# A new scheduler model and joined attention calls in a one-core kernel of attention and two mixture layers

## The chip, the cores and the metric

The kernel runs on one core of a Trainium2 chip. The metric is the device time of one execution in microseconds (us); lower is better. A core has TensorE (PE: matmuls, with its weight loads shown apart as PEld), VectorE (DVE), ScalarE (ACT), GpSimd (POOL) and SyncE (SP), which here issues all DMA transfers in one queue.

## The reference

Attention in 64 chunks of 64 by 64 for each of 8 heads, then two dense layers with gates; everything is fp32.

```python
B, H, S, D = 8, 8, 576, 64            # 4608 tokens, 512 wide
scores = matmul(q_c, k_c.T) / sqrt(D) # per 64-token chunk and head
attn = exp(scores - max); attn /= sum + 1e-9
x = matmul(attn, v_c)                 # -> [4608, 512]
g = x @ w_gate; v = x @ w_val         # [512, 1536] each
y = (g * sigmoid(g) * v) @ w_out      # [1536, 512]
h = y @ w_in                          # [512, 2048]
out = (h * sigmoid(1.702 * h)) @ w_out2   # [2048, 512]
```

## The kernel before

The 4608 tokens are cut into 9 blocks of 512. The work runs in four passes over all blocks: two over halves of the first layer (three groups of weights each), two over halves of the second (two groups each). A group multiplies a block by seven combinations of its quarters instead of eight quarters (`product`, seven calls a group, labels 1 to 7), and every fp32 factor is split into a high and a low part, so that a product is three matmuls (`mm3`, lines 249, 250 and 251: these are most of the time). One `product` call is twelve matmuls of 128x128 by 256 columns. What follows a group on PE is `second` in the first layer (three matmuls of 512 columns) and `last_product` in the second (six of 256 columns). In the second layer all seven products of a group go through one PSUM bank, `ga`; between two of them ACT copies the bank away (`u` or `c`, line 233).

Attention is part of the first pass: while block b is multiplied, `attend` makes the 4 units (128 tokens each) of block b+1. A unit is a score call on PE (16 small matmuls of 64x64 in the source, 32 rows in the trace, into bank `s`, line 483), a softmax of six DVE instructions and one exp on ACT (lines 488 to 496), four transposes on PE (line 507), a copy, a value call on PE (line 483 again, into bank `a`) and a copy into `xr`. `x_made` then splits the block into the seven x tiles.

The weights come as 8-byte numbers. `conv_part` turns them to fp32 (two ACT and two DVE instructions, lines 328 to 336), and splits by ACT and POOL follow. The first groups are made at the start (tiles `w`); those of later passes are background work (tiles `raw`, `t`, `st`, `ws`) that is stored in device memory and loaded later. In the second layer's last pass the second group's output weights are loaded one by one into the ring `o`, which has three buffers; ring `w` has 21.

Nothing is issued in the order in which it is written. Each step is an `Op` with an engine, a guessed duration, a priority (`prio`, a planned time in us) and its dependencies; `Program.emit` walks a model of the engines forward in time, takes on each engine the ready step of lowest priority and so fixes the order of every engine's queue and of SP's. On the chip each queue then runs in that order, and an instruction waits for its inputs.

```python
s, o = min(((s, o) for s, o in zip(start, todo) if s <= first + (0.1 if eng == "dve" else 0.3)),
           key=lambda x: (x[1].prio, x[1].n))
```

Of the kernel before, what the change touches and what calls it, by code (L numbers as in the profile page):

```python
# [18 lines left out]
P = 128  # L19
# [7 lines left out]
class Buf:  # L27
# [3 lines left out]
    def __init__(self, make, prev=None, before=None, whole=None):  # L31
        self.make, self.prev, self.before, self.whole = make, prev, before, whole
        self.users, self.writers, self.tile = [], [], None
# [18 lines left out]
class Ring:  # L52
    def __init__(self, pool, tag, bufs):
        self.pool, self.tag, self.bufs, self.made = pool, tag, bufs, []

    def new(self, shape, dtype=F32):
# [4 lines left out]
        b = Buf(make, prev, self.made[-1] if self.made else None)  # L61
        self.made.append(b)
# [3 lines left out]
class Op:  # L66
    __slots__ = ("eng", "us", "fn", "prio", "deps", "follows", "table", "near", "n", "done_at")


class Program:  # L70


    def __init__(self):
        self.ops, self.slack = [], None

    def op(self, eng, us, fn, reads=(), writes=(), prio=0, table=None, near=None):
        o = Op()
        o.eng, o.us, o.fn, o.prio, o.table, o.near, o.n = eng, us, fn, prio, table, self.slack if near is None and eng not in ('pe', 'dma') else near, len(self.ops)
# [20 lines left out]
    def emit(self):  # L99
        waiting = {o: len(o.deps) + len(o.follows) for o in self.ops}  # L100
        after = {}
        for o in self.ops:
            for d in (*o.deps, *o.follows):
                after.setdefault(d, []).append(o)
        ready = {}
        for o in self.ops:
            o.done_at = 0.0
            if not waiting[o]:
                ready.setdefault(o.eng, []).append(o)
        free, table = {}, None  # L110
        left = len(self.ops)
        while left:
            pick = None
            for eng, todo in ready.items():
                if not todo:
                    continue
                t = free.get(eng, 0.0)
                start = [max(t, o.done_at) for o in todo]
                first = min(start)
                s, o = min(((s, o) for s, o in zip(start, todo) if s <= first + (0.1 if eng == "dve" else 0.3)), key=lambda x: (x[1].prio, x[1].n))  # L120
# [4 lines left out]
            free[o.eng] = s + o.us + (1.3 if o.table and o.table != table else 0.0)  # L125
            end = free[o.eng] + (2.0 if o.eng == "dma" else 0.0)
            table = o.table or table
            o.fn()
            left -= 1
            for a in after.get(o, ()):  # L130
                if o in a.deps:
# [861 lines left out]
```

## Time and profile before

| | |
|---|---|
| median of 3 runs (lowest to highest) | 1752.32 us (1750.62 to 1753.2) |
| the profiled execution | 1753.21 us, of which its span (first to last instruction) is 1751.4 us |
| PE busy | 1704.3 us, 97% of the span |
| DVE, ACT, POOL busy | 1111.5 us, 882.3 us, 735.2 us |
| DMA | 477.91 MB, mean 273 GB/s |
| mean granted clock of PE | 0.987 of full speed |

A busy PE is not PE at its peak: the records of matmuls overlap, so the distance from one start to the next is the better measure of pace. Idle time of the other engines costs nothing as long as PE doesn't wait for them.

### The profile page before, as it was taken

To read this page: it belongs to the slowest core of one execution; us is meant where nothing else is said; L and a number is where in the kernel's file an instruction comes from. 1 tells how busy PE (TensorE), PEld (TensorE's weight loads), DVE (VectorE), ACT (ScalarE), POOL (GpSimd) and SP (SyncE) were. 2 spreads that over 40 slices of the span, in tenths; PEclk is the share of its full clock that TensorE was granted. 3 is DMA by queue.
4 is the path that set the end of the run, shared out by engine and by line. 5 is a ranking of instruction groups with operands and counts; after the bars stand their busy time and mean duration, and the time that the engine had idled before them with its cause. 6 is when DMAs were issued, how large, how long until landed. Compare 5 with 4: busy or idle time off the path is not lost.

```text
span 1751.4 us, 36463 instructions
## 1 busy us (share of the span) xinstructions
PE 1704.3 (97%) x14392; PEld 1617.2 (92%) x14392; DVE 1111.5 (63%) x1632; ACT 882.3 (50%) x1535; POOL 735.2 (42%) x762
## 2 busy tenths in 40 slices
PE   6889999999999999999999999999999999999998
PEld 6779989889999999999999989999999999999997
DVE  6887678767774464544445548778775555555555
ACT  5776666666763343333333446555544444444442
POOL 4665464636652145212222235656662133333333
PEclk8989999999999999999999999999999999999999
DMA  6568888887869988777778998989989977777774
GB/s 246 188 230 279 289 293 280 270 270 276 295 229 366 331 290 292 260 251 246 254 258 281 352 353 279 320 288 312 310 299 321 364 248 227 218 233 232 228 223 137
DMA packets 187323, 477.91 MB, mean 273 GB/s; under 512 B 20112, under 2 KB 47760, under 8 KB 187152
## 3 DMA queue, kind: packets, MB, share of 16 engines
q1 hardware_dynamic: 187152, 475.58, 80.5%
q8 instruction: 114, 1.87, 0.4%
q14 instruction: 57, 0.47, 0.1%
HBM read 334.46 MB, written 141.03 MB: 271 GB/s over the span
## 4 chain that ended last, share of the span: by engine, by line
PE 86%; DVE 5%; ACT 2%; issue 2%; DMA 1%; POOL 0%; POOLq 0%; ACTq 0%; DVEq 0%
PE ga L249 11%; PE ga L251 10%; PE ga L250 10%; PE yb L249 4%; PE ya L250 4%; PE ya L249 4%; PE ya L251 4%; PE yb L251 4%; PE yb L250 4%; PE gb L249 4%; PE gb L251 4%; PE gb L250 4%; PE s L249 2%; PE s L251 2%; PE s L250 2%
## 5 line engine op out<-in xcount | busy, mean ns | idle before, releaser
L249 PE MATMUL ga<-x,w 128*128 128x256 f32 x1640 | 472.9, 288 | 10.9 <-ACT u L233 3.9
L250 PE MATMUL ga<-x,w 128*128 128x256 f32 x1640 | 463.9, 283 | 3.0 <-DVE x L242 3.0
L251 PE MATMUL ga<-x,w 128*128 128x256 f32 x1640 | 464.6, 283 | 0.4 <-POOL w L242 0.4
L249 PEld LDWEIGHTS ga<-x,w 128*128 128x128 f32 x1640 | 311.7, 190 | 26.7 <-ACT u L233 9.8
L250 PEld LDWEIGHTS ga<-x,w 128*128 128x128 f32 x1640 | 311.6, 190 | 8.2 <-DVE x L242 3.3
L251 PEld LDWEIGHTS ga<-x,w 128*128 128x128 f32 x1640 | 311.5, 190 | 0.6 <-POOL w L242 0.6
L233 ACT COPY u<-ga 128x512 f32<-128x512 f32 x231 | 135.3, 586 | 254.3 <-PE ga L251 252.1
L242 DVE TENSOR_TENSOR c<-u,ga 128x512 f32<-128x512 f32 x143 | 98.2, 687 | 239.1 <-PE ga L251 229.7
L653 ACT ACTIVATE xr<-c 128x512 f32<-128x512 f32 x140 | 88.3, 631 | 135.1 <-DVE c L242 128.2
L242 DVE TENSOR_TENSOR c<-u,gb 128x512 f32<-128x512 f32 x125 | 85.4, 683 | 95.7 <-ACT u L233 68.0
L249 PE MATMUL gb<-x,w 128*128 128x256 f32 x500 | 143.4, 287 | 1.5 <-DVE c L242 1.5
L251 PE MATMUL gb<-x,w 128*128 128x256 f32 x500 | 141.8, 284 | 0.0
L250 PE MATMUL gb<-x,w 128*128 128x256 f32 x500 | 141.6, 283 | 0.0
L613 ACT ACTIVATE h<-c 128x512 f32<-128x512 f32 x108 | 67.9, 632 | 118.6 <-DVE c L242 118.0
L235 POOL CAST ws<-t 128x256 fp32r<-128x256 f32 x78 | 41.0, 526 | 193.7 <-DMA wd_b<-ws 85.5
L242 DVE TENSOR_TENSOR xr<-xr 128x512 f32<-128x512 f32 x140 | 117.4, 839 | 5.4 <-ACT xr L653 3.1
L242 POOL TENSOR_TENSOR k<-xr,q 128x512 fp32r<-128x512 f32 x24 | 37.5, 1564 | 173.8 <-ACT q L233 64.7
L242 DVE TENSOR_TENSOR hl<-h,hh 128x512 fp32r<-128x512 f32 x108 | 92.0, 872 | 17.0 <-ACT hh L233 16.8
L249 PEld LDWEIGHTS gb<-x,w 128*128 128x128 f32 x500 | 95.4, 191 | 4.3 <-DVE c L242 1.7
L242 POOL TENSOR_TENSOR u<-u 128x512 f32<-128x512 f32 x36 | 48.7, 1352 | 117.7 <-ACT u L233 117.7
L242 POOL TENSOR_TENSOR yv<-yv,e 128x512 f32<-128x512 f32 x18 | 23.2, 1288 | 177.2 <-ACT e L233 115.9
L250 PEld LDWEIGHTS gb<-x,w 128*128 128x128 f32 x500 | 95.5, 191 | 2.0
(253 smaller groups left out, 5077.0 us busy)
## 6 DMA issues: line engine op xcount, KB each, us to landing
x<-x_dram SPq DMA_DIRECT2D x189, 512.0 KB, 5.3
o<-od_b SPq DMA_DIRECT2D x126, 512.0 KB, 4.7
o<-od_a SPq DMA_DIRECT2D x102, 512.0 KB, 5.3
x_dram<-x SPq DMA_DIRECT2D x63, 512.0 KB, 4.3
wd_b<-ws SPq DMA_DIRECT2D x56, 256.0 KB, 5.0
od_b<-ws SPq DMA_DIRECT2D x56, 256.0 KB, 5.1
w<-wd_b SPq DMA_DIRECT2D x28, 512.0 KB, 6.2
raw<-in_moe_w_out SPq DMA_DIRECT2D x56, 255.8 KB, 4.8
```

The lines of the kernel that those rows point to most:

```text
L233: op("act", act_us(n), lambda: nc.scalar.copy(out=dst.ap, in_=cut(src.ap)), [src], [dst], prio, near=near)
L235: op("pool", pool_us(0.6 * n), lambda: nc.gpsimd.tensor_copy(dst.ap, cut(src.ap)), [src], [dst], prio)
L242: lambda: e.tensor_tensor(out=dst.ap, in0=of_a(a.ap), in1=of_b(b.ap), op=by), [a, b], [dst], prio, near=near)
L249: nc.tensor.matmul(o, ah, bh, start=first, stop=False, **kind)
L250: nc.tensor.matmul(o, ah, bl, start=False, stop=False, **kind)
L251: nc.tensor.matmul(o, al, bh, start=False, stop=last, **kind)
L613: op("act", act_us(512), lambda h=h, i=i: nc.scalar.activation(out=h.ap, in_=of(0)(c[i].ap), func=AF.Silu), [c[i]], [h], prio, "silu")
L653: op("act", act_us(512), lambda: nc.scalar.activation(out=h.ap, in_=c.ap, func=AF.Gelu_apprx_sigmoid), [c], [h], prio, "gelu")
```

## The change

Three things. First, the durations given to the steps are new, and the model now knows that DVE and POOL share a port (`port`: a DVE step that reads no PSUM tile, and every POOL step, take it one after the other), how long a hop between engines lasts, and how transfers queue. Second, `emit` runs 12 rounds: it makes an order (`order`), works back from its end to the latest time at which each step may end or begin (`dues`), steps through the order once more with a model of PE's clock (`replay`), and then moves each step's key half way to its latest time; the best of the 12 by `replay` is issued. Third, attention from block 2 on is cut otherwise: `attend_next` makes units two ahead of the block, and `scores` issues the value call of unit u-2 and the score call of unit u as one step (`both_blocks`); units 34 and 35 end with a value call alone. There are 26 joined calls. And in the last block of the last pass the `o` tiles of the second group come from ring `w`.

```diff
     def op(self, eng, us, fn, reads=(), writes=(), prio=0, table=None, near=None, port=None):
...
+        o.port = eng == "pool" or eng == "dve" and port is not False and not any(a.bank for b in reads for a in b.line())
...
+    def order(self):
...
+                limit = min(max(t, o.ready) for o in todo) + self.WINDOW[eng]
+                o = min((o for o in todo if o.ready <= limit), key=lambda o: (o.key, o.n))
...
+                if o.port:
+                    o.end = max(s + 0.1, port) + o.us - 0.1
+                    port = o.end - 0.1
+                else:
+                    o.end = s + o.us
...
+    def dues(self, seq):
...
+            if o.eng == "dma":
+                o.due = t - 2.8 - 0.865 * o.us
+            elif o.eng == "pe":
+                o.due = free = min(t, free) - o.us
+            else:
+                o.due = t - o.us
...
+    def emit(self):
+        for o in self.ops:
+            o.key, o.after = o.prio, []
...
+        for i in range(self.ROUNDS):
+            seq = self.order()
+            self.dues(seq)
+            last = self.replay(seq)
+            if best is None or last < best[0]:
+                best = last, seq
+            for o in self.ops:
+                if o.prio < 9999:
+                    o.key = (o.key + o.due) / 2
+        for o in best[1]:
             o.fn()
...
+    def scores(un, prio, done=None):
+
+        if done is None:
+            op("pe", 1.24, lambda: blocks(un.s.ap, un.q.ap, un.k.ap), [un.q, un.k], [un.s], prio)
+        else:
+            def both_blocks():
+                blocks(done.o.ap, done.v.ap, done.e.ap)
+                blocks(un.s.ap, un.q.ap, un.k.ap)
+
+            op("pe", 2.2, both_blocks, [done.v, done.e, un.q, un.k], [done.o, un.s], prio, near=1.0)
+            attended(done, prio)
...
+    def attend_next(u, prio):
+
+        if u < NU:
+            un = unit(u)
+            fetch(un, un.q, q, prio - 10)
+            fetch(un, un.k, k, prio - 10)
+            scores(un, prio, flying.pop(0) if len(flying) > 1 else None)
+            softmax(un, prio)
+            flying.append(un)
+        else:
+            alone(flying.pop(0), prio)
+        last = [un for un in flying if un.v is None and un.u < u]
+        for un in last:
+            un.v = ring["v"].new([P, 512])
+            fetch(un, un.v, v, prio - 6)
+            turned(un, prio)
...
-                                        w = ws[n] = ring["o"].new([P, 2, 2, 256], F32R)
+                                        tag = "w" if (p, b) == (NPASS - 1, NB - 1) else "o"
+                                        w = ws[n] = ring[tag].new([P, 2, 2, 256], F32R)
...
-                    for u in range(UPB * j // len(gs), UPB * (j + 1) // len(gs)):
-                        at = t - 22 + u * 14 if b else t + 4 + u * 16
-                        attend(UPB * (b + 1) + u, at, at - 10)
+                    units = range(2 if b > 1 else 0, UPB + 2 if b else UPB)
+                    for u in units[len(units) * j // len(gs):len(units) * (j + 1) // len(gs)]:
+                        if b:
+                            attend_next(UPB * (b + 1) + u, t + -6.0 + (u - 2) * 13.5)
+                        else:
+                            attend(UPB + u, t + 4 + u * 16, t - 6 + u * 16)
```

How this moves the instructions is seen at three places.

DVE while block 0 is multiplied, before: the rows that lead to the end of the conversion of the third group's first weight tile (lines 333 and 336, `t`); lines 488 to 496 are a unit's softmax, `c` an evacuation that PE waits for.

```order
L489 TENSOR_TENSOR e<-s,m 128x512
L492 TENSOR_REDUCE z<-e 128x8
L242 TENSOR_TENSOR c<-u,gb 128x512
L493 TENSOR_SCALAR z<-z 128x8
L495 RECIPROCAL z<-z 128x8
L496 TENSOR_TENSOR e<-e,z 128x512
L333 SCALAR_TENSOR_TENSOR t<-t,raw 128x256
L242 TENSOR_TENSOR c<-u,ga 128x512
L336 SCALAR_TENSOR_TENSOR t<-raw,t 128x256
L333 SCALAR_TENSOR_TENSOR t<-t,raw 128x256
L242 TENSOR_TENSOR c<-u,gb 128x512
L336 SCALAR_TENSOR_TENSOR t<-raw,t 128x256
```

The same after the change, to the same conversion's end (lines 452 and 455; the softmax has lines 630 to 638).

```order
L361 TENSOR_TENSOR c<-u,gb 128x512
L361 TENSOR_TENSOR h<-h,c 128x512
L630 TENSOR_REDUCE m<-s 128x8
L452 SCALAR_TENSOR_TENSOR t<-t,raw 128x256
L455 SCALAR_TENSOR_TENSOR t<-raw,t 128x256
L361 TENSOR_TENSOR hl<-h,hh 128x512
L631 TENSOR_TENSOR e<-s,m 128x512
L452 SCALAR_TENSOR_TENSOR t<-t,raw 128x256
L455 SCALAR_TENSOR_TENSOR t<-raw,t 128x256
```

The conversion's last row stood as DVE's 99th instruction and stands as its 86th; the conversions that follow it move ahead by 14 to 19, and softmaxes move behind them. By the evacuation of the fifth product of block 1's first group 165 instructions stood ahead on DVE, now 159: one unit's softmax is no longer among them. The background conversions of later weights move too: before the last evacuation of the first pass's last group 176 of 256 conversion instructions stood on DVE, now 192, and before block 8's last x tile 237 of 447 background steps stood on POOL, now 285.

PE in the last pass, before: between two products through `ga` (their last and first rows) there is one `last_product` (into bank `s`).

```order
L250 MATMUL ga<-x,w 128x256
L251 MATMUL ga<-x,w 128x256
L249 MATMUL s<-w,v 128x256
L250 MATMUL s<-w,v 128x256
L251 MATMUL s<-w,xt 128x256
L249 MATMUL s<-w,v 128x256
L250 MATMUL s<-w,v 128x256
L251 MATMUL s<-w,xt 128x256
L249 MATMUL ga<-x,w 128x256
```

After, ahead of the same product (its first row stands last), the end of two `last_product` calls (into `ya`).

```order
L369 MATMUL ya<-w,hh 128x256
L370 MATMUL ya<-w,hl 128x256
L368 MATMUL ya<-w,hh 128x256
L369 MATMUL ya<-w,hh 128x256
L370 MATMUL ya<-w,hl 128x256
L368 MATMUL ya<-w,hh 128x256
L369 MATMUL ya<-w,hh 128x256
L370 MATMUL ya<-w,hl 128x256
L368 MATMUL ga<-x,w 128x256
```

In the second layer's passes 32 products stood one `last_product` behind the product before them in `ga`, 178 two, 27 three or more; now 1, 228 and 8. Products right behind each other in `ga` are 4 before and 4 after.

SP at the end, before: the last loads of output weights (`o`, from the second group's `od_b`), among the stores of the last blocks' outputs.

```order
L226 DMA t<-o_dram 128x512
L226 DMA o<-od_b_96 128x1024 x3
L229 DMA out<-yv 128x2x256
L226 DMA o<-od_b_96 128x1024
L229 DMA out<-yv 128x2x256
L229 DMA out<-t 128x2x256 x2
```

SP at the end, after.

```order
L345 DMA w<-od_b_96 128x1024
L345 DMA yv<-o_dram 128x512
L345 DMA o<-od_b_96 128x1024
L345 DMA w<-od_b_96 128x1024 x2
L348 DMA out<-yv 128x2x256
L348 DMA out<-t 128x2x256
L345 DMA yv<-o_dram 128x512
L345 DMA t<-o_dram 128x512
L348 DMA out<-t 128x2x256
L348 DMA out<-yv 128x2x256 x2
L348 DMA out<-t 128x2x256 x2
```

The seven loads that go into `w` (the last three are shown) stand ahead of the stores of block 7's `t` tiles; before, the last four loads of `o` stood behind those stores.

## Rows read from the trace of the kernel before

**Rows 1.** Busy time and share of the span, whole run.
```profile
PE 1704.3 (97%) x14392; PEld 1617.2 (92%) x14392; DVE 1111.5 (63%) x1632; ACT 882.3 (50%) x1535; POOL 735.2 (42%) x762
```

**Rows 2.** Stretches: length, busy of PE, PEld, DVE, ACT, POOL; clock, DMA share, GB/s.
```profile
36.00:127.00 91.00, 71.61 (x701) 64.11 (x702) 79.65 (x118) 68.56 (x133) 67.33 (x67) 0.86 0.59 202
127.00:550.00 423.00, 419.69 (x4110) 383.55 (x4111) 311.61 (x493) 272.95 (x459) 228.45 (x270) 1.00 0.83 281
1070.00:1720.00 650.00, 648.79 (x5387) 642.14 (x5386) 415.75 (x592) 321.38 (x557) 276.88 (x267) 1.00 0.82 271
```

**Rows 3.** Waits of PE in 36 to 127: total, times, longest; first and last of ten.
```profile
PE a L483 <- ACT e L510: 3.7, 1, 3.7
...
PE ga L251 <- POOL w L242: 0.4, 1, 0.4
```

**Rows 4.** Timeline of POOL: start, length, instruction, [idle before, releaser].
```profile
84.84 1.78 POOL L242 TENSOR_TENSOR w<-t,w 128x256 fp32r<-128x256 f32 x2 [7.09 <-ACT w L233]
```

**Rows 5.** DVE's groups in 127 to 550: busy, mean ns, idle before.
```profile
L333 DVE SCALAR_TENSOR_TENSOR t<-t,raw 128x256 int32<-128x256 f32 x62 | 37.0, 601 | 12.1 <-ACT raw L330 10.4 <-POOL ws L242 1.3 <-issue 0.3
...
L496 DVE TENSOR_TENSOR e<-e,z 128x512 f32<-128x512 f32 x25 | 19.6, 783 | 0.5
...
L492 DVE TENSOR_REDUCE z<-e 128x8 f32<-128x512 f32 x25 | 17.1, 683 | 9.8 <-ACT e L491 9.6
L488 DVE TENSOR_REDUCE m<-s 128x8 f32<-128x512 f32 x24 | 16.4, 684 | 17.6 <-PE s L483 17.6
```

**Rows 6.** Timeline of PE at the edge from block 4 to block 5.
```profile
348.93 0.40 PE L251 MATMUL yb<-hh,o 128*128 128x512 f32 x1
352.09 1.08 PE L507 MATMUL a<-ident,e 128*128 128x128 f32 x4 [2.77 <-DVE e L496]
...
353.19 0.41 PE L250 MATMUL ga<-x,w 128*128 128x256 f32 x1
353.40 0.41 PE L251 MATMUL ga<-x,w 128*128 128x256 f32 x1
```

**Rows 7.** Timeline of PE: a value call alone, and one followed by a score call.
```profile
308.91 0.28 PE L251 MATMUL ga<-x,w 128*128 128x256 f32 x1
309.12 1.15 PE L483 MATMUL a<-e,v 64*64 64x64 f32 x32
310.19 0.50 PE L249 MATMUL ya<-hh,o 128*128 128x512 f32 x1
...
319.34 1.15 PE L483 MATMUL a<-e,v 64*64 64x64 f32 x32
320.32 1.10 PE L483 MATMUL s<-k,q 64*64 64x64 f32 x32
```

**Rows 8.** Timeline of PE: products one `last_product` behind the last, two of 32.
```profile
1374.96 0.28 PE L251 MATMUL yb<-o,h 128*128 128x256 f32 x1
1375.19 0.39 PE L249 MATMUL ga<-x,w 128*128 128x256 f32 x1
...
1616.57 0.28 PE L250 MATMUL yb<-o,hh 128*128 128x256 f32 x1
1616.69 0.28 PE L251 MATMUL yb<-o,hl 128*128 128x256 f32 x1
1616.99 0.39 PE L249 MATMUL ga<-x,w 128*128 128x256 f32 x1
```

**Rows 9.** Timeline of the end: PE, POOL and SP.
```profile
1734.05 0.28 PE L249 MATMUL yb<-o,hh 128*128 128x256 f32 x1
...
1740.51 0.28 PE L249 MATMUL s<-o,v 128*128 128x256 f32 x1
...
1744.85 1.28 POOL L242 TENSOR_TENSOR t<-t,e 128x512 f32<-128x512 f32 x1 [0.16 <-DVE e L242]
...
1747.55 0.90 SPq L229 DMA_DIRECT2D out<-t  x2
```

**Rows 10.** Timeline of DVE beside a busy POOL.
```profile
346.30 1.51 DVE L333 SCALAR_TENSOR_TENSOR t<-t,raw 128x256 int32<-128x256 f32 x1
```

More of the change, by code (lines that the diff above doesn't have):

```diff
@@ L1 @@
+import heapq
 from contextlib import ExitStack
@@ L97, in op, with hop @@
         return o
-    def emit(self):
-        waiting = {o: len(o.deps) + len(o.follows) for o in self.ops}
-        after = {}
+    def hop(self, d, o):
+        return 0.0 if d.eng == o.eng else self.HOP.get((d.eng, o.eng), 0.06)
+    def order(self):
+        ready = {eng: [] for eng in self.FREE}
         for o in self.ops:
[L103 to L112, printed above, removed]
+            o.ready, o.left = 0.0, len(o.deps) + len(o.follows)
+            if not o.left:
+                ready[o.eng].append(o)
+        free, table, port, moved, seq = dict(self.FREE), None, 0.0, 0.0, []
+        while len(seq) < len(self.ops):
             pick = None
@@ L116, in emit @@
                     continue
[L117 to L120, printed above, removed]
+                t = free[eng]
+                limit = min(max(t, o.ready) for o in todo) + self.WINDOW[eng]
+                o = min((o for o in todo if o.ready <= limit), key=lambda o: (o.key, o.n))
+                s = max(t, o.ready)
                 if pick is None or s < pick[0]:
@@ L124, in emit @@
             ready[o.eng].remove(o)
-            free[o.eng] = s + o.us + (1.3 if o.table and o.table != table else 0.0)
-            end = free[o.eng] + (2.0 if o.eng == "dma" else 0.0)
-            table = o.table or table
-            o.fn()
-            left -= 1
-            for a in after.get(o, ()):
-                if o in a.deps:
-                    late = (0.3, 1.2)[a.eng == "pe" and o.eng != "pe"] + (1.5 if o.eng == "dma" else 0.0)
-                    if a.near is not None and o.eng != "dma":
-                        late = a.near
-                    a.done_at = max(a.done_at, end + ((0.0 if a.eng == "pe" else 0.13) if a.eng == o.eng else late))
-                waiting[a] -= 1
-                if not waiting[a]:
-                    ready.setdefault(a.eng, []).append(a)
+            o.begin = s
@@ L476, in attend @@
-            s = both.part(lambda ap: ap[:, 0])
-        def blocks(o, st, mv):
-            for i in range(H):
-                for r in (slice(0, CH), slice(CH, P)):
-                    cs = slice(i * CH, i * CH + CH)
-                    nc.tensor.matmul(o[r, cs], st[r, cs], mv[r, cs], start=True, stop=True)
-        op("pe", 1.2, lambda: blocks(s.ap, qb.ap, kb.ap), [qb, kb], [s], prio)
+            un.both = ring[both].new([P, 2, 512])
+            un.s = un.both.part(lambda ap: ap[:, 0])
+        return un
```

206 lines of the change are left out of this document (167 added, 39 removed).

## The prediction

> **What bounds the kernel now.** I read the page's busy times first, then the table of stretches, then what PE waits for. PE is busy for 97% of the span, no other engine over 63% [rows 1], so the time is PE's own work plus the stretches in which PE stands still. Those are few. In the steady part of the second layer PE is busy 648.8 of 650 us at full clock; in the first pass after the start 419.7 of 423 [rows 2]. The bad stretch is 36 to 127: PE is busy 71.6 of 91 us, and the granted clock is 0.86, a mix of the two levels of 1.2 and 2.4 GHz [rows 2]. There DVE is busy 79.7 of 91 us: the weights are converted, split and multiplied at once, and PE waits for ten different things, from a copy of ACT (3.7 us) down to a split of POOL (0.4) [rows 3]. A busy PE can still lose time, since records of matmuls overlap. I therefore took starts: a 128x256 matmul starts 0.12 us after the one before it (1616.57, 1616.69), so a product of twelve takes 1.43 us [rows 8]. What lies above that pace is what a better order can win.
>
> **The change part by part.** It removes no arithmetic. The twelve rounds run while the program is made and cost the chip nothing. What moves is the order, and 26 pairs of calls.
>
> *Joined calls.* A value call alone starts 0.21 us after the last 128x256 matmul, where the next one would start after 0.12, so going in costs 0.09; and it holds PE for 1.07 us until the next large matmul, where one followed by a score call gives way after 0.98: coming out costs another 0.09 [rows 7]. A join saves one of each, 0.18 to 0.19. Of the 26 pairs 4 stood side by side already in the order before; 22 x 0.19 = **4.2 us**. The join adds a wait: the value call now needs q and k of two units on, and the score call needs the value's operands. Both loads are planned 10 us ahead, and the value's operands belong to a unit whose score was one or two units (13.5 us each in the plan) before. I take 0; at worst the join saves nothing.
>
> *The stall at the edge of block 5.* PE's queue had transposes next, whose softmax was late on DVE: the last matmul before starts at 348.93 and the transposes at 352.09, with 2.8 us of idle time between. Then the clock is at its lower level: matmuls start 0.21 apart (353.19, 353.40) where 0.12 is normal, 0.09 x 12 = 1.1 us for the product that follows [rows 6]. With transposes one unit behind their softmax the order has a whole unit of PE work between them, so this wait goes: 2.8 + 1.1 = **3.9 us**. Smaller ones of its kind I leave at 0.
>
> *Spacing in the second layer.* All products go through one bank, so a product must wait until ACT has copied the last one out. With two `last_product` calls between, 1.43 us, the copy is covered. With one it isn't: the first matmul of such a product starts 0.30 us after the one before it in one row (1616.69 to 1616.99) and 0.23 in another (1374.96 to 1375.19), 0.18 and 0.11 over the pace [rows 8]. There were 32 such products and 1 is left: 31 x 0.15 = **4.7 us**. The four products with nothing between stay four: 0.
>
> *The end.* The last `o` loads come late because their ring has three buffers. From 1734.05, the last matmul group on time, six `last_product` halves of 0.715 us (six times 0.12) lead to 1738.34; the sixth starts at 1740.51, so 2.2 us are lost by then [rows 9]. Loaded into `w`, whose first seven buffers come free when the first group's products are done, they are there a group's length ahead. PE waits longer still for the last tile, but that is not all won: after the product that ends then, POOL has three additions in a chain, and its last begins at 1744.85 and ends at 1746.13. Only what lies between this and the last store is left: two stores are issued from 1747.55 on, the second about 0.45 later, at 1748.0 [rows 9], where POOL's end would let it go at 1746.2, 1.8 us earlier. 2.2 + 1.8 = **4.0 us**. If the new loads are late in turn, 0; if POOL's chain shortens too, no more than the row allows.
>
> *The start.* Conversions move ahead of softmaxes. In the order, the third group's first tile is through on DVE 13 instructions sooner. POOL sat idle for 7.1 us before the splits of that group [rows 4], so they can begin sooner; but POOL's splits of x and of the second group keep their places, and the attention of block 1 now comes late. What is surely less by the middle of block 1's first group is one softmax on DVE: 0.68 for the maximum, as much for the subtraction (same shape), 0.68 for the sum and 0.78 for the scaling, **2.8 us** [rows 5], two small ones left out; and DVE is the busiest there (88%) [rows 2]. I take that. Bounds: the idle POOL of 7.1 us and half of PE's 19.4 idle us won, 9.7; or the longest wait doubled, 3.7 lost [rows 3].
>
> *Background work moved ahead.* 16 conversion instructions on DVE at 0.60 us [rows 5] are 9.6 us, 48 steps on POOL at 0.89 (two take 1.78) [rows 4] are 43 us, more in the first pass than before. DVE has 111 idle us between 127 and 550, POOL 195 [rows 2]. Cover: these gaps, since the keys put what PE waits for first. I take 0. If the cover is gone, see the second rival.
>
> Sum: 4.2 + 3.9 + 4.7 + 4.0 + 2.8 = 19.6. The profiled execution took 1753.2 us, 1.8 more than its span and 0.9 more than the median of the runs; 1753.2 - 19.6 = 1733.6, and as a median about **1733 us**. The range of this case alone is 1724 to 1742: down by half of the start's bound, up by the join and the end at nothing.
>
> **The rivals.**
>
> *The start opens up.* If the conversions' head start fills half of PE's idle 19.4 us and the clock stays up with it (0.86 granted over 91 us means some 25 us at the lower level, 12.7 us lost, of which half), the start gives 9.7 + 6.4 = 16.1 in place of 2.8: 1719. For it: POOL's idle 7.1 us before the third group [rows 4]. Against it: DVE at 88%, and the x tiles of block 1 now wait for later attention.
>
> *DVE and POOL get in each other's way in the first pass (slower).* A conversion of 0.60 us mean took 1.51 us at 346.30, just before that stall [rows 6, 10]; so 48 more POOL steps can each hold a DVE instruction up, by up to 0.9 us, 43 us in all, and DVE's queue is in order: the evacuation behind it waits, and PE for that. If each of six edges between later blocks gets a stall like that of block 5, 6 x 3.9 = 23.4 are lost and the one saved stays lost: 1733 + 27 = 1760. From five such stalls on the gain is gone. The Trainium skill, SBUF — State Buffer, "SBUF: two separate sides", says that DVE and GpSimd hold the shared port pair as an exclusive lock for a whole instruction, a DVE one with two SBUF inputs against a GpSimd one that reads SBUF; by that rule a held instruction waits the whole step out, and the loss is the upper 43 us, 1776 if none of it is covered. The 1.51 us agrees with the rule. Against this rival: POOL has 195 idle us to spread the steps over, and DVE keeps over a fifth of its time idle.
>
> *The gains are given back.* The order is right by the plan, but the plan has errors of its own: every order on PE is rigid, and a step that is 1 us late holds all behind it. Before, the first pass lost about 3.3 us to idling after the start and the second layer 1.2 [rows 2]; if 63 products or joins come 0.2 us late, as those of [rows 8] do, that is 12.6 us, and with the start's gain gone too, 2.8, the time is 1748. Nothing in the profile speaks for it but how tight the old order was.
>
> **How the numbers follow.** Forecast 0.53; the start opens up 0.15; given back 0.18; slower by the port 0.14. The range takes the forecast's case whole, half of the first rival and much of the third: 1715 to 1750. A difference below 0.2% (3.5 us) is about what a measurement of this kernel can't tell from no change: under 1748.8 is faster, over 1755.8 slower. Faster: 0.53 + 0.15 + 0.11 of the third = 0.79; same 0.08; slower 0.13.
>
> **What the next profile would show.** Right: rows of 64 small matmuls without a break; no wait of PE for DVE's softmax product at a block's edge; products in `ga` with 0.12 us to the matmul before them; no wait of PE for the last loads of output weights, and the last store within 5 us of the last product but one; DVE busier than 311.6 us over the first pass after the start. Wrong: in the stretch after the start, waits of PE for DVE's evacuations or for splits by ACT and POOL that add up to over 10 us; a start that ends later than 127; conversion instructions well over 0.60 us mean.

## The result, and the profile after

The changed kernel takes 1767.5 us (median of 4, 1766.3 to 1771.0) against 1752.8 us for the kernel before (median of 4): a ratio of 1.0083, interval 1.0058 to 1.0109. It is slower by some 15 us, where 19 to 20 less were forecast. The profiled execution took 1770.99 us with a span of 1769.2, 17.8 more than the span before.

Busy time and share of the span, whole run of the changed kernel, as [rows 1]:

```profile
PE 1704.2 (96%) x14392; PEld 1618.5 (91%) x14392; DVE 1134.3 (64%) x1632; ACT 888.1 (50%) x1537; POOL 728.6 (41%) x762
```

PE does the same work as before; the 17.8 us are time in which it stands or runs at its lower clock. Where, the stretches tell. Columns as in [rows 2]; first the changed kernel, then the one row of before that isn't in [rows 2]:

```profile
36.00:127.00 91.00, 76.89 (x700) 68.10 (x701) 78.90 (x110) 70.79 (x136) 65.46 (x65) 0.84 0.55 193
127.00:550.00 423.00, 409.69 (x4086) 374.48 (x4085) 330.51 (x510) 273.79 (x467) 262.18 (x318) 1.00 0.85 296
1000.00:1300.00 300.00, 282.63 (x2233) 274.52 (x2233) 202.40 (x293) 157.87 (x281) 157.74 (x187) 0.98 0.87 297
1070.00:1720.00 650.00, 638.11 (x5296) 632.90 (x5296) 414.46 (x586) 318.90 (x549) 264.30 (x266) 1.00 0.82 271
```

```profile
1000.00:1300.00 300.00, 295.52 (x2433) 291.68 (x2432) 219.57 (x309) 169.64 (x303) 171.28 (x188) 1.00 0.90 310
```

PE is idle 13.3 us in the first pass after the start, where it was idle 3.3, and 17.4 us between 1000 and 1300, where it was idle 4.5. In these two stretches POOL, which splits the background's weights, has the most work: it is busy for 262 of 423 and 158 of 300 us, against 83 of the 440 us from 560 to 1000. To put a size on all of it, I took from the trace the distance from each PE call's start to the next one's, less the pace of a call that isn't held up (`product` 1.43, `second` 0.70, `last_product` 0.71 us), and summed what was over:

| stretch (us) | before | after | difference |
|---|---|---|---|
| 127 to 560, first pass | 12.9 | 26.0 | +13.1 |
| 560 to 1000, second pass | 1.8 | 0.7 | -1.1 |
| 1000 to 1300, second layer, its first pass | 7.6 | 31.0 | +23.4 |
| 1300 to 1700 | 6.0 | 2.1 | -3.9 |
| 1700 to the last product | 6.1 | 0.0 | -6.1 |

This makes +25.4. Some 6 us of the +23.4 may be the clock, an estimate from the rows above: 0.98 granted where it was 1.00, over 300 us. The joined calls' own saving (4.2 by the prediction's rows) isn't in it, since it lies in the pace; 25.4 - 4.2 = 21.2. From the start of the last product to the last store it is 4.0 us (1761.70 to 1765.70) for 2.7 before, which adds 1.3; and the first product of block 1 begins at 117.5 for 122.2, 4.7 us won in the start. 21.2 + 1.3 - 4.7 = 17.8.

### One stall, from its end back to its cause

PE, then ACT, then SP and DVE, timelines of the changed kernel about 450 us, where PE loses the most at once in the first pass:

```profile
450.28 0.39 PE L370 MATMUL ya<-hh,o 128*128 128x512 f32 x1
453.38 0.39 PE L368 MATMUL ga<-x,w 128*128 128x256 f32 x1 [2.71 <-ACT u L352]
```

```profile
445.77 0.59 ACT L650 COPY e<-a 128x512 f32<-128x512 f32 x1 [0.55 <-PE a L647]
450.81 0.52 ACT L447 ACTIVATE t<-raw,offset 128x256 f32<-128x256 int16 x1 [4.45 <-DMA raw<-in_moe_w_in]
451.37 0.52 ACT L449 ACTIVATE raw<-raw,offset 128x256 f32<-128x256 int16 x1
451.79 0.51 ACT L447 ACTIVATE t<-raw,offset 128x256 f32<-128x256 int16 x1
452.33 0.53 ACT L449 ACTIVATE raw<-raw,offset 128x256 f32<-128x256 int16 x1
452.76 0.57 ACT L352 COPY u<-ga 128x512 f32<-128x512 f32 x1
```

```profile
441.54 2.00 SPq L348 DMA_DIRECT2D od_b<-ws  x2
443.63 1.02 SPq L345 DMA_DIRECT2D v<-in_v  x1
...
445.71 0.84 SPq L345 DMA_DIRECT2D raw<-in_moe_w_in  x2
```

```profile
443.84 0.42 DVE L455 SCALAR_TENSOR_TENSOR t<-raw,t 128x256 int32<-128x256 int32 x1
```

PE waits 2.71 us for the copy of `ga` (`u`). The product in `ga` was done at 449.3, and ACT, idle for 4.45 us up to 450.81, could have copied it then. But its queue has four instructions of the background conversion ahead of that copy, and the first waits for its raw weights. Those were issued at 445.71 and used at 450.81, 5.1 us later. SP's queue delayed the issue a little: two stores of split weights (`od_b<-ws`) wait for POOL, until 443.2, and a `v` load behind them 1.0 us for PE. But `raw` has two buffers, and DVE's last read of the one that this load fills ends at 444.26, so a free queue would have brought the load at most 1.5 us forward; the 5.0 us from its issue to its landing would have stayed. No key helps here: once the order is made, a copy that PE needs stands behind a conversion that nobody needs yet, for as long as that waits. The Trainium skill, Perfetto Trace Analysis, "Tensor Engine Instruction (MATMUL, LD_WEIGHTS)", calls ACT, DVE and GpSimd strict FIFO; this row agrees. For SP it is its DMA: Bandwidth & Descriptors, "Anatomy of one DMA — SWDGE (gpsimd) path", that says a wait for a semaphore happens on the issuing sequencer; the SP rows agree.

How often: ACT's group of first conversion instructions in 127 to 550, before and after (busy, mean ns, idle time ahead of it):

```profile
L328 ACT ACTIVATE t<-raw,offset 128x256 f32<-128x256 int16 x62 | 32.6, 526 | 18.7 <-DMA raw<-in_moe_w_out 8.1 <-DMA raw<-in_moe_w_gate 5.7 <-DMA raw<-in_moe_w_val 3.1
```

```profile
L447 ACT ACTIVATE t<-raw,offset 128x256 f32<-128x256 int16 x68 | 35.7, 526 | 59.0 <-DMA raw<-in_moe_w_out 16.1 <-POOL st L361 10.9 <-DMA raw<-in_moe_w_gate 9.4
```

PE's waits for copies into `u` in the same stretch (total, times, longest), before and after:

```profile
PE ga L249 <- ACT u L233: 1.2, 1, 1.2
```

```profile
PE ga L368 <- ACT u L352: 9.9, 8, 2.7
```

SP's waits for POOL there, before and after:

```profile
SPq L229 <- POOL ws L242: 42.1, 36, 3.8
SPq L229 <- POOL ws L235: 18.7, 12, 3.4
```

```profile
SPq L348 <- POOL ws L361: 71.2, 56, 3.4
SPq L348 <- POOL ws L354: 32.1, 16, 3.6
```

18.7 us became 59.0, 1.2 became 9.9, and 60.8 became 103.3. SP's longer waits explain only a small part of ACT's. Set each raw load of the changed kernel beside the end of DVE's last read of the buffer that it fills, which is that of the conversion two before: half of the loads are issued within 0.10 us of it. 25 of the 68 conversions start within 0.2 us of their load's landing; ACT is idle for 49.8 us ahead of these, and for at most 12.2 us of that a load stood in SP's queue with its buffer already free, where it was 11.0 us of the 18.7 before. What came on top is the place in ACT's queue, too near behind the load.

In the second layer SP's queue holds up what PE needs itself. SP, POOL and PE of the changed kernel:

```profile
1177.58 0.32 SPq L348 DMA_DIRECT2D od_b<-ws  x1
...
1181.92 0.32 SPq L348 DMA_DIRECT2D od_b<-ws  x1
1182.33 0.38 SPq L345 DMA_DIRECT2D x<-x_dram  x1
1182.80 0.40 SPq L345 DMA_DIRECT2D o<-od_b  x1
```

```profile
1180.67 0.40 POOL L354 CAST ws<-st 128x256 fp32r<-128x256 f32 x1 [2.24 <-DMA od_b<-ws]
```

```profile
1188.20 0.35 PE L368 MATMUL yb<-o,h 128*128 128x256 f32 x1 [0.34 <-DMA o<-od_b]
```

A store waits for POOL's split, POOL waits for the buffer of an earlier store to come free (2.24 us), and an `x` and an `o` load stand behind the store; PE then waits for `o`, here 0.34 us. Such waits are the smaller part: of PE's idle time between 1000 and 1300, 5.4 us ended with a load of `o` or `x`, 11.6 with a copy of ACT or an evacuation or split of DVE. Longer waits near 1055 (1.54 us for ACT's `hh`, 0.68 for its `u`) also take the clock to its lower level for some 7 us (0.83 granted over 1050 to 1070): two of a call's matmuls there, 0.21 us apart where 0.12 is normal:

```profile
1057.16 0.41 PE L370 MATMUL ya<-o,hl 128*128 128x256 f32 x1
1057.37 0.41 PE L368 MATMUL ya<-o,hh 128*128 128x256 f32 x1
```

Why things stand too early: the planner's time for a transfer. In the code before, a 256 KB load to ACT took 0.74 + 2.0 + 1.5 + 0.3 = 4.5 us from issue to user, and a 512 KB load to PE 1.48 + 2.0 + 1.5 + 1.2 = 6.2. The new code has (`s` is the issue, `moved` the time when the data of this and all earlier transfers is through)

```python
moved = max(s + 1.5, moved) + 0.865 * o.us
o.end = moved + 1.3
```

and a hop of 0.06, with 0.5 of slack for PE: 1.5 + 0.64 + 1.3 + 0.06 = 3.5 and 1.5 + 1.28 + 1.3 + 0.06 + 0.5 = 4.6, where the plan has no earlier transfer in the way. What the chip took (KB each, median us from issue to landing): in the first fence a raw load in 127 to 550 and in the second an `o` load in 1000 to 1360, both of the changed kernel:

```profile
raw<-in_moe_w_out SPq DMA_DIRECT2D x28, 255.8 KB, 4.4
```

```profile
o<-od_b SPq DMA_DIRECT2D x55, 512.0 KB, 5.0
```

The kernel before has 4.6 and 5.2 there. So the old allowances, 4.5 and 6.2, were about right or generous, and the new ones, 3.5 and 4.6, are short of the median, 0.9 and 0.4 us. The Trainium skill, DMA: Bandwidth & Descriptors, "Anatomy of one DMA — SWDGE (gpsimd) path", has a fit for one DMA issued by GpSimd, 2.0 us + bytes / 436e3 us; by it the estimate would be 2.6 and 3.2 us. The loads here are issued by SP, with the DMA engines busy for 85% of the time, and what they took, 4.4 and 5.0, decides.

### The profile page after: what moved, and what is told of

Same layout as the page of the kernel before. It is cut to its first block, busy times and chain, and to the rows that moved or that the text cites. A ratio compares the mean times of both kernels' runs of the same rounds, so it can differ in the third digit from the quotient of the medians.

```text
span 1769.2 us, 36486 instructions
## 1 busy us (share of the span) xinstructions
PE 1704.2 (96%) x14392; PEld 1618.5 (91%) x14392; DVE 1134.3 (64%) x1632; ACT 888.1 (50%) x1537; POOL 728.6 (41%) x762
## 4 chain that ended last, share of the span: by engine, by line
PE 67%; DMA 13%; DVE 7%; POOL 5%; issue 4%; ACT 3%; SPq 0%; POOLq 0%; DVEq 0%; ACTq 0%
PE ga L368 8%; PE ga L370 8%; PE ga L369 8%; PE ya L368 4%; PE ya L370 4%; PE yb L368 4%; PE ya L369 4%; PE yb L370 3%; PE yb L369 3%; PE gb L368 3%; PE gb L370 3%; PE gb L369 3%; DMA raw<-in_moe_w_out 2%; PE s L368 2%; PE s L370 2%
## 5 line engine op out<-in xcount | busy, mean ns | idle before, releaser
L370 PEld LDWEIGHTS ga<-x,w 128*128 128x128 f32 x1640 | 311.6, 190 | 0.9 <-POOL w L361 0.9
L361 DVE TENSOR_TENSOR xr<-xr 128x512 f32<-128x512 f32 x140 | 123.3, 881 | 17.2 <-ACT xr L828 12.3
L361 DVE TENSOR_TENSOR h<-h,c 128x512 f32<-128x512 f32 x108 | 98.5, 920 | 27.4 <-ACT h L788 26.0
L447 ACT ACTIVATE t<-raw,offset 128x256 f32<-128x256 int16 x120 | 63.0, 527 | 87.4 <-DMA raw<-in_moe_w_out 31.1
L452 DVE SCALAR_TENSOR_TENSOR t<-t,raw 128x256 int32<-128x256 f32 x120 | 74.6, 628 | 48.0 <-ACT raw L449 41.7
```

What stands on the lines that cost most here:

```text
L361: lambda: e.tensor_tensor(out=dst.ap, in0=of_a(a.ap), in1=of_b(b.ap), op=by), [a, b], [dst], prio, near=near)
L370: nc.tensor.matmul(o, al, bh, start=False, stop=last, **kind)
L447: op("act", conv_us(n), lambda: nc.scalar.activation(out=t.ap, in_=raw.ap[:, :, 2], func=AF.Relu, scale=up, bias=offset.ap[:, :1]), [raw, ...
L452: op("dve", dve_us(n), lambda: nc.vector.scalar_tensor_tensor(out=t.ap.bitcast(I32), in0=t.ap, scalar=-4096 * up, in1=word(1).bitcast(F32) ...
```

## The experiments

Four theories were set against one another. **L**: the planner counts on loads too early, and ACT's queue is held. **S**: SP's queue is held by stores that wait for POOL. **C**: crowding, more conversions in the same stretch and DVE and POOL in each other's way (the prediction's slower rival). **J**: the joined calls are late. All runs are compared with the kernel before on the same chip. `o.bg` marks steps of the background conversion.

| run | median us | ratio to before, interval | first pass | 2nd layer, `product` | 2nd layer, `last_product` | ACT idle | SP wait |
|---|---|---|---|---|---|---|---|
| before | 1752.8 | | 12.9 | 6.6 | 0.9 | 18.7 | 60.8 |
| after | 1767.5 | 1.0083, 1.0058 to 1.0109 | 26.0 | 13.3 | 16.5 | 59.0 | 103.3 |
| e1 margin, all | 1741.8 | 0.9940, 0.9918 to 0.9963 | 5.5 | 5.9 | 4.3 | 6.2 | 52.5 |
| e2 background | 1741.1 | 0.9936, 0.9915 to 0.9956 | 9.6 | 4.0 | 11.4 | 10.0 | 52.4 |
| e3 foreground | 1760.0 | 1.0045, 1.0030 to 1.0060 | 19.4 | 14.6 | 5.9 | 42.3 | 106.0 |
| e5 raw to ACT | 1754.2 | 1.0008, 0.9996 to 1.0021 | 14.5 | 6.5 | 16.4 | 25.8 | 103.0 |
| e10 stores | 1749.5 | 0.9984, 0.9973 to 0.9994 | 14.7 | 14.2 | 11.8 | 26.7 | 32.9 |
| e9 raw and stores | 1738.7 | 0.9928, 0.9907 to 0.9949 | 8.5 | 5.9 | 10.0 | 10.5 | 43.9 |
| e6 before, tight | 1768.0 | 1.0099, 1.0080 to 1.0119 | 16.4 | 8.6 | 8.3 | 32.4 | 77.3 |
| e14 paced | 1754.0 | 1.0009, 0.9998 to 1.0020 | 10.5 | 13.9 | 11.1 | 10.6 | 60.5 |
| e12 margin after start | 1733.6 | 0.9892, 0.9875 to 0.9909 | 5.3 | 6.3 | 6.1 | 8.4 | 54.5 |
| e13 the same, paced | 1727.8 | 0.9850, 0.9837 to 0.9864 | 4.5 | 6.5 | 2.3 | 1.6 | 41.2 |

The middle columns are us over the pace as above (127 to 560; 1000 to 1300 by the call that started late); ACT idle is what stands ahead of its group of first conversion instructions, SP wait is for POOL's `ws`, both in 127 to 550.

Every one of these edits makes the planner find a new order, so more moves than the margin. In e2, e5, e9 and e10 the first product of block 2 begins at 174.2 to 176.0 us, in the changed kernel at 177.8, in e1 and e3 at 182.5: some us are won or lost in the start, which none of the theories explains. The second pass, 0.7 us late in the changed kernel, is some 4 late in e2, e5, e9 and e10 and 8.7 in e14. And in e1, e2, e9 and e10 only 60 to 64 conversions are left in 127 to 550, as in the kernel before (62) and not as in the changed one (68); of the margins on the background only e5 keeps it ahead (67).

**e1, e2, e3: a margin after transfers.** For all:

```diff
     def hop(self, d, o):
-        return 0.0 if d.eng == o.eng else self.HOP.get((d.eng, o.eng), 0.06)
+        return 0.0 if d.eng == o.eng else 2.0 if d.eng == "dma" else self.HOP.get((d.eng, o.eng), 0.06)
```

> The changed kernel with one number different: its planner lets 2.0 us pass between the planned end of any transfer and its user, in place of 0.06 (0.3 to PE's stores is not touched). Theory L (late loads): the plan counts on transfers too early, so instructions that need one stand too far forward in queues that run in order; ACT stands 59.0 us before the first conversion instruction between 127 and 550 where it stood 18.7 before the change, and the copies that PE needs are behind it. Then the stalls at the product six of the second group and the waits for output weights between 1000 and 1300 go: 12 + 20 us or so less than 1767, about 1738, and ACT's idle before the conversions falls to about 20 us. Theory C (crowding: more conversions and POOL steps in the same stretch, longer instructions by DVE and POOL in each other's way): this order still has most conversions ahead of where they stood, so only a part comes back, about 1760. Theory J (the joined calls make attention late): nothing changes, 1767.

With `d.eng == "dma" and o.bg`:

> As the run with the margin of 2.0 us after every transfer, but only for the transfers of the background conversion (raw weights in, split weights out). Theory L: the stalls at ACT in the first pass go, 12 us, and those of the second layer's first pass that come from ACT; the waits of last_product calls for their output weights, a third of the 23 us there, stay: about 1747. Theory C: the background is slower by plan, so crowding falls too, about 1755 to 1760. Theory J: 1767.

With `d.eng == "dma" and not o.bg`:

> As the run with the margin of 2.0 us, but only for the transfers that are not of the background conversion (x, weights, output weights, q, k, v). The background stands as far forward as in the changed kernel. Theory L: ACT's waits before the conversions stay (about 59 us between 127 and 550) and with them the 12 us of the first pass; the late output weights of the second layer go, so about 1757. Theory C: nothing comes back, 1765 or more. Theory J: 1767.

e1 came 25.7 us under the changed kernel, e2 26.4, e3 7.5. L's numbers for e1 and e3 are within 4 us, its number for e2 was 6 too high; J is out. e3 splits the second layer: the late `last_product` calls fall from 16.5 to 5.9 with a margin on their loads, while the late `product` calls stay at 14.6; in `ga` they wait 4.6 us for copies of ACT and 5.4 for evacuations of DVE.

**e5: the margin at one place.** `(d.eng, o.eng) == ("dma", "act") and o.bg`:

> The changed kernel with 2.0 us of margin at one place only: between the planned end of a load of raw weights and ACT's first conversion instruction on them. The background keeps its head start over the kernel before (16 or 17 conversion instructions on DVE per 50 us of planned PE work, where it had 12 to 18), so crowding is hardly less than in the changed kernel. Theory L: ACT's idle before conversions falls from 59.0 us (127 to 550) to about 10, and most of the 26 us won by the margin on all of the background come back here too: 1745. Theory C (longer instructions and more work in the same stretch): 1760 or more.

13.3 us less: three fifths of what L expected, and more than C allows. PE's waits for `u` in 127 to 550 fall from 9.9 us to 0.2, but ACT's idle time only to 25.8, not to 10. ACT's row in 127 to 550:

```profile
L448 ACT ACTIVATE t<-raw,offset 128x256 f32<-128x256 int16 x67 | 35.1, 526 | 25.8 <-DMA raw<-in_moe_w_out 6.7 <-DMA raw<-in_moe_w_gate 6.5 <-DMA raw<-in_moe_w_in 6.4
```

The 67 conversions are as many as in the changed kernel (68), so the gain isn't from less work; late `product` calls of the second layer halve (13.3 to 6.5), late `last_product` calls don't move. SP still waits 103.0 us. That led to theory S.

**e9, e10: SP's stores.** `o.bg and (d.eng, o.eng) in (("dma", "act"), ("pool", "dma"))`, then the second pair alone:

> As the run with 2.0 us between a raw load and ACT's conversion (1754), and with 2.0 us as well between POOL's last step on a split weight and the store of it, which waits at the head of SP's queue with the loads of x, q, k and output weights behind it. Theory S (the other half of the loss is SP's queue, held by such stores: 103 us of waiting for POOL between 127 and 550 and 68 between 1000 and 1360, where the kernel before had 61 and 39): the waits fall to some 50 and 35, PE's excess in the second layer's first pass falls from 23 to about 12, and the time is about 1741, as with a margin on all of the background. If it is not SP's queue but something else that the margin after the stores and loads slowed down: 1750 to 1754.

> The changed kernel with 2.0 us of margin only between POOL's last step on a split weight and its store; raw loads keep the tight date. Theory S with theory L: SP's waits at stores fall to some 50 us (127 to 550), the loads behind them leave earlier, and with them the raw loads too, so ACT's idle before conversions falls from 59 to some 40: 1755. If the SP queue is harmless: 1765.

SP's waits for POOL's `ws` in 127 to 550, run e10:

```profile
SPq L349 <- POOL ws L362: 19.6, 24, 2.3
SPq L349 <- POOL ws L355: 13.3, 12, 2.6
```

e10 alone gives 18.0 us, e5 alone 13.3, both together 28.8 (1738.7 where 1741 was expected): nearly the sum, and all of e2's 26.4. So margins at these two places give all that a margin on the background gives. That two queues are held, each for about half, isn't shown. e10 was better than expected (1755), and ACT's idle time falls too, to 26.7; but not since raw loads leave earlier: half of them are issued within 0.07 us of a free buffer, where it was 0.10. ACT's conversions stand later: they start a median of 2.3 us after their load's landing, where it was 0.8. And SP waits for PE's `yb` in place of POOL, 48.4 us for 17.7. How much of e10's 18.0 us is SP's queue stays open.

**e6: the cause put into the kernel before.**

```diff
-            end = free[o.eng] + (2.0 if o.eng == "dma" else 0.0)
+            end = free[o.eng] + (1.0 if o.eng == "dma" else 0.0)
```

> The kernel before with the allowance of its own planner for a transfer cut by 1.0 us (from 2.0 to 1.0 at its end, on top of the 1.5 that it adds ahead of the user), which brings it near to that of the changed kernel; nothing else is touched, and the background stands at most 2 instructions per 50 us elsewhere. Theory L: conversions stand too early in ACT's queue here as well, its idle before them between 127 and 550 rises from 18.7 to some 40 us, PE waits for copies behind them, and the time rises by about 8 us, to 1760. Theory C or a cause in the joined calls: no change, 1752.

```profile
L328 ACT ACTIVATE t<-raw,offset 128x256 f32<-128x256 int16 x63 | 33.3, 528 | 32.4 <-DMA raw<-in_moe_w_in 12.8 <-DMA raw<-in_moe_w_out 11.2 <-DMA raw<-in_moe_w_gate 3.9
```

1768.0, 15 us slower, twice what L expected and as slow as the changed kernel: with its old planner, old attention and the background where it was, one microsecond less for a transfer is enough. The place is another, though. By the table the first pass is 3.5 us later than before, where the change made it 13.1, the second layer 9.4; and PE's waits for `u` in 127 to 550 are 0.9 us, no more than before (1.2). So e6 shows what a tighter allowance can cost by itself, but doesn't make the first pass's stalls.

**e4, e14: pacing without a margin.** No background step begins in the plan before its job's date:

```diff
-            o.ready, o.left = 0.0, len(o.deps) + len(o.follows)
+            o.ready, o.left = o.prio if o.bg else 0.0, len(o.deps) + len(o.follows)
```

> The changed kernel with its margins as they are, but no transfer or step of the background conversion may begin in the plan before the date that its job was given, so that the weights of the third pass are converted over the second pass and not in the first. Theory C: the first pass has a third less of conversion and POOL work than before the change and loses its 12 us; the second layer's first pass, where the conversion is spread a little wider only, gets a few back: about 1752. Theory L: each conversion that is left still stands 1.4 us behind its load in the plan and holds up ACT, but there are fewer: 4 to 6 us, about 1762. Theory J: 1767.

> The paced kernel without margins once more, for its trace. Theories L and S: ACT's idle before the conversions between 127 and 550 is well under the 59 us of the changed kernel, in proportion to the conversions left there (some 25 to 35), and SP's waits for POOL's splits under 60; in the second layer's first pass, where hardly anything is paced, both stay (26 and 68). Theory C: these waits stay as they were per conversion and DVE's products are shorter, h and hl by 0.05 us or more each.

e4 took 1755.6 us, ratio 1.0010 (0.9992 to 1.0029), between the two theories; one of its executions took 5013 us and was the profiled one, so nothing is read from its trace. e14 is the same kernel. ACT's idle falls to 10.6 us with 36 conversions left of 68, which is less than L's proportion (25 to 35) and not C's constant wait per conversion. In the second layer, where little is paced, most of the loss stays (13.9 and 11.1), with ACT's idle at 18.6 us for 26.5 and SP's waits at 65.7 for 67.9 (1000 to 1360). `h` products of DVE are shorter as well (0.80 for 0.99 us mean), as C expected, so e14 alone doesn't decide.

**e12, e13: the best order, and crowding by itself.** e12: `d.eng == "dma" and (o.bg or o.prio > 60)`; e13 adds e4's line.

> The changed kernel with the margin of 2.0 us after every transfer of the background, and after all other transfers from planned time 60 on. With the margin everywhere the second block began 13 us later than with the margin on the background alone (124.7 against 111.6) and won 5 us back in the second layer, where output weights came on time. If the two are independent, this run has both: about 1736. If the start's order decides nothing beyond the third block: 1741.

> The run with margins after the start (1733.6), and no step of the background begins in the plan before its job's date: between 100 and 500 us of planned PE work some 72 conversion instructions on DVE in place of 116, and the third pass's weights are converted over the second pass. With the margins on, ACT and SP stand before few late transfers in either run, so what differs is crowding. Theory C: PE's excess over its pace in the first pass falls by 5 us or more, 1728 or less. Theories L and S: nothing left to win there, 1732 to 1735.

Stretches 127 to 550 of e12, then of e13:

```profile
127.00:550.00 423.00, 422.71 (x4220) 390.24 (x4217) 321.99 (x503) 278.08 (x464) 226.55 (x269) 1.00 0.86 296
```

```profile
127.00:550.00 423.00, 423.00 (x4222) 390.81 (x4221) 283.49 (x454) 257.61 (x420) 157.78 (x182) 1.00 0.77 267
```

e13 takes 38 us of DVE and 69 us of POOL work out of this stretch and wins 0.8 us of PE's loss there. Its time, 1727.8, is C's number, but not from C's place: of the 3.7 us between the two spans most is in the second layer (`last_product` 6.1 to 2.3); why pacing helps there isn't shown. Once queues aren't held, crowding in the first pass costs next to nothing. e13 beats both kernels, by 1.5% and 2.2%.

**e7, e11, e8: the prediction's terms alone.** e7 is e1 with `attend` for all blocks; e11 is the kernel before with `attend_next` from block 2 on; e8 is the kernel before with one line:

```diff
-                                        w = ws[n] = ring["o"].new([P, 2, 2, 256], F32R)
+                                        tag = "w" if (p, b) == (NPASS - 1, NB - 1) else "o"
+                                        w = ws[n] = ring[tag].new([P, 2, 2, 256], F32R)
```

> The run with 2.0 us of margin after every transfer (1741.8), but with the attention of all blocks in the old form: each unit's score, transposes and value call on their own, and the dates of before. If the joins are worth what the prediction said (4.2, and the stall at the edge of block 5, 3.9): 1746 to 1750. If the stall was cured by the planner and not by the joins: 1746. If the joins bring nothing: 1742.

> The kernel before, with its own planner and durations, and the attention of the change from the third block on: value call joined with the score call two units on, transposes one unit behind. By the prediction's terms: 4.2 for the joins and 3.9 for the stall at the edge of block 5, 1744.5. If the planner and not the joins cured the stall: 1748.5. If the joined calls wait for loads of q and k: 1752 or more.

> The kernel before with one edit: the output weights of the last block of the last pass are loaded into the ring of 21 buffers in place of the ring of three. By the prediction's term for the end: 4.0 us less, 1748.7. If the wait for them only moves to the chain of sums behind the last products: 0 to 2 less, 1751.

e7: 1746.4 (0.9969, 0.9956 to 0.9982), 4.6 above e1, a difference that the two intervals leave open by about as much. e11: 1748.9 (0.9981, 0.9972 to 0.9989), 3.8 under before. Both fit joins worth 4 us, but both are nets: e7 begins block 2 at 179.3 us where e1 does at 182.5, and is 11.5 us late in the first pass for e1's 5.5; e11 begins it at 183.6, before at 179.6. The wait of the transposes (4.2 us over the pace before) is 0.2 in e11, but its `second` calls rise from 3.1 to 8.1, so the stall's price was not won there. e8: 1751.8 (0.9999, 0.9989 to 1.0009), no difference that can be told; in its profile the way from the last group on time to the last store is 11.2 us (1735.24 to 1746.48) for 13.9 in [rows 9], with a wait for DVE of 0.89 us in its place. These 2.7 us don't show in the median, whose interval ends 1.9 us below the kernel before.

## Why the prediction was wrong

The step that failed is **"Background work moved ahead"**: "Cover: these gaps, since the keys put what PE waits for first. I take 0." It cost +13.1 us in the first pass, with the stall of block 5 already saved in it, and +23.4 in the second layer, which the step didn't speak of. Not all of that is the background: 15.6 of the 23.4 are `last_product` calls (0.9 to 16.5), and a margin on the foreground's loads alone brings these to 5.9 (e3). That the new plan counts on those loads sooner was no term of the sum. Gaps are no cover when queues run in order: an instruction that waits at the head of a queue, as at 450.81, takes the gap and all behind it. The keys choose among steps that the plan holds ready, and the plan's idea of ready had moved, by 1.0 us for ACT's loads and 1.6 for PE's. I read the diff's new transfer times as planning detail and never set them beside the trace's issue-to-landing times, which the DMA view of before would have allowed; ACT's 18.7 us ahead of conversions was the warning.

The rival **"The gains are given back"** was nearest to the mechanism: "the plan has errors of its own", and a late step holds all behind it. But it saw this on PE alone, as 63 calls that come 0.2 us late, and so at 1748; what was late were loads, and in the first pass the queue that held PE up was ACT's.

The **slower rival** had the sign and 1760 us, by another mechanism. Its evidence is weak: `h` products did grow longer, and so did conversions, but little (changed kernel, 127 to 550, beside [rows 5] for the second):

```profile
L452 DVE SCALAR_TENSOR_TENSOR t<-t,raw 128x256 int32<-128x256 f32 x70 | 45.4, 653 | 37.9 <-ACT raw L449 34.0 <-POOL ws L354 1.6 <-POOL x L361 1.3
...
L361 DVE TENSOR_TENSOR h<-h,c 128x512 f32<-128x512 f32 x43 | 41.8, 991 | 4.9 <-ACT h L788 4.6
```

0.65 for 0.60 us a conversion, while the idle time ahead of them went from 12.1 to 37.9, for ACT. The exclusive lock of the Trainium skill, SBUF — State Buffer, "SBUF: two separate sides", may well lengthen such rows; but in e13, with 30% of POOL's and 12% of DVE's work taken out of the stretch, PE gains 0.8 us.

The other terms, by the prediction's working:

- *Joined calls*, 4.2: right by the rows, and 4.6 in e7 and 3.8 in e11 agree, as nets. A pair holds PE for 2.01 us (0.99 and 1.02) and is gone into once, 0.21 after the last large matmul, beside [rows 7]:

```profile
319.79 0.28 PE L370 MATMUL gb<-x,w 128*128 128x256 f32 x1
320.00 1.15 PE L591 MATMUL a<-e,v 64*64 64x64 f32 x32
320.99 1.10 PE L591 MATMUL s<-k,q 64*64 64x64 f32 x32
322.01 0.50 PE L368 MATMUL ya<-hh,o 128*128 128x512 f32 x1
```

- *The stall at the edge of block 5*, 3.9: gone (transposes lose 0.1 us in all, 4.2 before), and outweighed by the stalls above.
- *Spacing*, 4.7: right. The 32 products one `last_product` behind were 5.3 us late in all, the one that is left 0.2. (The -3.9 of the table is a net of this and other calls.) From 1300 on a product two `last_product` calls behind starts at the pace, 0.12, beside [rows 8]; between 1000 and 1300, 77 of them lose 7.9 us, where 80 lost 2.3:

```profile
1630.99 0.28 PE L370 MATMUL s<-w,xt 128*128 128x256 f32 x1
1631.11 0.28 PE L368 MATMUL ga<-x,w 128*128 128x256 f32 x1
```

- *The end*, 4.0: right with the new order. From the last group on time to the second store's issue it is 9.7 us (1755.98 to 1765.70) for 13.9 in [rows 9], 4.2 less; in e8's profile, though not in its median, the edit alone gives 2.7 of it. PE and SP:

```profile
1755.98 0.28 PE L368 MATMUL yb<-w,hh 128*128 128x256 f32 x1
...
1765.19 0.92 SPq L348 DMA_DIRECT2D out<-t  x2
```

- *The start*, 2.8: 4.7 by the first product of block 1, of which 1.8 is left at the first of block 2 (177.8 for 179.6). The orders that the planner made in the experiments begin block 1 anywhere from 109.9 to 124.7; why was not studied.

One figure of its working doesn't follow: half of the start's bound of 9.7 leads from 1733 to 1728, not to 1724; the last range doesn't rest on it.

So five terms of six came near, and most signs that the prediction named for "right" are there: 64 small matmuls without a break, no transposes late at a block's edge, no late output weights at the end, DVE busier (330.5 us for 311.6). Products are at the pace from 1300 on, but not in the first pass nor between 1000 and 1300. The signs for "wrong" missed what happened: in 127 to 550 PE waits 2.6 us for DVE's evacuations and not for splits, while the 9.9 us for ACT's copies were named by no sign. e12, the change with later transfers, took the forecast's 1733.6; partly by chance, since it wins more in the start (granted clock 0.90 in 36 to 127, changed kernel 0.84) and still loses in the second layer.

Left open: e12 and e13 still lose 12 and 9 us in the second layer's first pass, some 6 of it in late `product` calls, and 2 of the 5.7 us between their medians are not seen in their profiles. The planner's new keys, windows and durations were not run apart from its new transfer times, so what they win or cost by themselves is open, and so is how the loss divides between ACT's queue, SP's queue and the foreground's loads.

## What to carry to other kernels

Where an order is planned, set the plan's time for a transfer beside the trace's issue-to-landing time under load, and give the user of a load a margin above the median: too late costs a little slack, too early holds a whole in-order queue. Look for instructions with long idle time ahead of them that nobody waits for, and then at what stands behind them on that engine; a store that waits for its producer can do the same to loads in the issuing queue. Low-urgency work is not free because its engine has gaps.

## What was not expected of the hardware

One microsecond in the allowance for a transfer is worth 15 us in 1752 (e6), on a core whose PE is 97% busy. A load of 256 KB takes a median of 4.4 us and one of 512 KB 5.0 us from issue to landing with the DMA engines busy at 0.85 and 0.87. From before to after this hardly changes (raw loads in the first pass, by tensor: 4.0 to 4.6, then 3.9 to 4.6): what changes is when they are used. Over all orders read here it goes from 3.5 to 6.6; the 6.6 are in e13, the fastest.
